# The last two half experts of a dense layer: 1024 tokens through seven block products instead of plain matmuls, the last 512 tokens plain at the end

## The chip, the core and the metric

The kernel runs on one core of a Trainium2 chip. Five engines work side by side, each through its own instructions in the order in which they stand: TensorE (PE) multiplies into PSUM banks, VectorE (DVE), ScalarE (ACT) and GpSimd (POOL) work on elements, and SP, ACT and POOL issue DMA transfers. The metric is the time of one execution on the device in microseconds (us); the less the better.

## The reference, cut to what matters

Three parts follow one another: a local attention with summary keys, a mixture of eight experts in which every token goes through every expert, and a second mixture in which each token goes through one expert. The change is in the second part and in the start of the third.

```python
x = attention(q, k, v)                    # 1536 tokens x 512
# dense part: P is the Sinkhorn-scaled softmax of the gate
for e in range(8):                        # w1[e]: 512 x 1024, w2[e]: 1024 x 512
    out += P[:, e:e + 1] * (np.maximum(x @ w1[e], 0) @ w2[e])
x = out
# routed part
e_idx = np.argmax(x @ w_gate, axis=1)
for e in range(8):                        # only the tokens that chose e
    ye = np.maximum(x[mask] @ w1[e], 0) @ w2[e]
    out[mask] = gate_w[mask, None] * eom[mask, e, None] * ye
```

## The kernel before, in words

All products are made of three matmuls each: every float32 operand is split into a high part, which is rounded (a cast on ACT, L472, L584 or L1755), and a low part, which is the rest (a subtraction on DVE, L473, L585 or L1758), and hi\*hi, lo\*hi and hi\*lo are added in one PSUM bank.

**The dense part** (`DenseMoe`) takes the eight experts in 16 halves `hx` of 512 hidden features. It handles halves 0 and 1, and 14 and 15, in a plain way: for groups of 384 tokens, `mm1` makes the hidden features (four blocks of 128, each 12 matmuls of 384 columns, L605), ACT takes their relu and high part (L612), DVE the low part (L613), and `mm2` makes one output tile of 128 tokens from 12 matmuls of 512 columns (L625), which DVE adds to that tile's sums (`acc`, L637). Halves 2 to 13 go in a Strassen scheme: sets of 512 tokens, both products of each set cut into 2 x 2 blocks of 256, and seven block products instead of eight. The seven of the first product are `s1` to `s7`, those of the second `z1` to `z7`; each is 12 matmuls of 256 columns for each of two halves (L678), 168 matmuls per set for both products. `TURNS` interleaves the `z` products of one set with the `s` products of the next. Weights and tokens are added up before they are multiplied: `weights` makes the sums and splits them, and `FIRSTS` (W1) and `SECONDS` (W2) say at which turn. The sums of the output leave SBUF at once: POOL issues DMAs that add them to a table in DRAM (`x2d<-acc`, L842).

After the last set its seven `z` products run between the plain matmuls of half 14; then the tiles are fetched back to SBUF (`reload`, L653) and get the plain contributions of halves 14 and 15. `done(i)` follows the last of tile i.

**The routed part** begins inside that. `Routing` has per tile a `flip` (PE transposes, L1289, copied to `r_xt`), the `logits` (L1298, copied to `r_lg`, L1299), and per run of tiles `choose`, `ranks`, `place`, `gates`, which sort the tokens by expert. Constants (`r_ilo` to `r_desc`, L1246) come from POOL's iotas (L1244). Two *early* slots of 128 tokens are chosen from the first `TILES` tiles, so that their work fills the end of the dense part; the rest is planned when all 12 tiles are there. `invert` (L1465) turns ranks into token numbers, POOL gathers the rows (`xg`, L1764), `flip_x` transposes them (L1782), and a slot goes through `mm1` and `mm2` of its expert (L1791) with weights of 1 MB loaded to a ring of three buffers `raw` (L1741). The function `late_steps` says in which order and with how many steps between them these run, `merge` threads them between the steps of the dense part.

## Time and profile before

| what | value |
|---|---|
| time, median of 3 runs | 1302.24 us (1301.32 to 1302.99) |
| time of the profiled execution | 1303.32 us |
| its span | 1301.2 us |
| PE busy | 1281.5 us (98%) |
| DVE, ACT, POOL busy | 840.3, 731.4, 356.5 us |

The span is from the first to the last instruction in the trace; 2.1 us of the profiled execution lie around it. The busy share of an engine counts the time in which it had an instruction in work.

### The profile page before, as it was taken

How to read it: one execution, taken by the hardware profiler on the slowest of the kernel's cores; microseconds unless marked ns; L12 is line 12 of the kernel's file. 1: busy time of each engine (PE TensorE's matmuls, PEld its weight loads, DVE VectorE, ACT ScalarE, POOL GpSimd, SP SyncE). 2: the span in 40 equal slices, each digit the busy share in tenths (PEclk: the TensorE clock that was granted, in tenths of full speed). 3: DMA queues.
4: the chain of work that ended last, by engine and by line, in shares of the span. 5: the costliest groups of instructions: out<-in, count | busy, mean ns of one | idle time of the engine just before them, and what ended most of it. 6: DMA issues, size and time to landing. Idle time of an engine off the chain costs nothing. (4 is left out here: it accounts for less than half of the span.)

```text
span 1301.2 us, 26457 instructions
## 1 busy us (share of the span) xinstructions
PE 1281.5 (98%) x10041; PEld 1205.7 (93%) x10041; DVE 840.3 (65%) x1673; ACT 731.4 (56%) x1511; POOL 356.5 (27%) x369
## 2 busy tenths in 40 slices
PE   8999999999999999999999999999999999999997
PEld 7888888999999999999999999999999998888886
DVE  6754595777778687787777787867643347514261
ACT  5764323667767677677677776767632114324362
POOL 6652005323324242333232332422210001111110
PEclk9999999999999999999999999999999999999999
DMA  9850227778889798888897888979571128114450
GB/s 218 194 123 10 89 106 283 197 192 179 194 192 198 182 211 170 226 167 211 186 200 186 177 199 192 204 176 218 81 181 34 65 82 277 64 56 141 142 194 22
DMA packets 163176, 208.84 MB, mean 160 GB/s; under 512 B 47199, under 2 KB 96351, under 8 KB 163040
## 3 DMA queue, kind: packets, MB, share of 16 engines
q1 hardware_dynamic: 114192, 138.36, 34.4%
q0 software_dynamic: 48848, 68.70, 29.7%
q8 instruction: 81, 1.33, 0.4%
q14 instruction: 55, 0.45, 0.1%
HBM read 151.18 MB, written 56.62 MB: 160 GB/s over the span
## 5 line engine op out<-in xcount | busy, mean ns | idle before, releaser
L842 POOL DMA_DIRECT2D x2d<-acc x144 | 172.8, 1243 | 453.7 <-ACT acc L837 169.6
L678 PE MATMUL bank<-hi,hlo 128*128 128x256 f32 x672 | 190.0, 283 | 0.3 <-DVE hlo L713 0.3
L678 PE MATMUL bank<-lo,hhi 128*128 128x256 f32 x672 | 189.9, 283 | 0.0
L678 PE MATMUL bank<-hi,hhi 128*128 128x256 f32 x672 | 189.5, 282 | 0.0
L678 PE MATMUL bank<-Tlo,hi 128*128 128x256 f32 x576 | 162.9, 283 | 0.0
L678 PE MATMUL bank<-Thi,lo 128*128 128x256 f32 x576 | 162.6, 282 | 0.0
L678 PE MATMUL bank<-Thi,hi 128*128 128x256 f32 x576 | 162.1, 281 | 0.0
L678 PE MATMUL bank<-hi,acc 128*128 128x256 f32 x672 | 133.7, 282 | 0.0
L678 PEld LDWEIGHTS bank<-hi,hhi 128*128 128x128 f32 x672 | 127.9, 190 | 0.3 <-DVE acc L862 0.2
L678 PEld LDWEIGHTS bank<-hi,hlo 128*128 128x128 f32 x672 | 127.4, 190 | 0.5 <-DVE hlo L713 0.5
L678 PEld LDWEIGHTS bank<-lo,hhi 128*128 128x128 f32 x672 | 127.4, 190 | 0.0
L678 PE MATMUL bank<-xhi,hi 128*128 128x256 f32 x432 | 121.4, 281 | 0.7 <-ACT t L772 0.7
L678 PE MATMUL bank<-xlo,hi 128*128 128x256 f32 x432 | 121.4, 281 | 0.0
L678 PE MATMUL bank<-xhi,lo 128*128 128x256 f32 x432 | 121.3, 281 | 0.0
L678 PEld LDWEIGHTS bank<-hi,acc 128*128 128x128 f32 x672 | 109.8, 190 | 0.0
L678 PEld LDWEIGHTS bank<-Thi,hi 128*128 128x128 f32 x576 | 109.0, 189 | 0.0
L678 PEld LDWEIGHTS bank<-Thi,lo 128*128 128x128 f32 x576 | 108.6, 188 | 0.0
L678 PEld LDWEIGHTS bank<-Tlo,hi 128*128 128x128 f32 x576 | 108.3, 188 | 0.0
L713 DVE TENSOR_TENSOR hlo<-t,hhi 128x512 fp32r<-128x512 f32 x144 | 97.0, 685 | 14.2 <-ACT hhi L705 13.4
L705 ACT CAST hhi<-t 128x512 fp32r<-128x512 f32 x144 | 88.1, 619 | 23.7 <-DVE t L807 17.4
L837 ACT ACTIVATE acc<-acc,P 128x256 f32<-128x256 f32 x216 | 96.7, 502 | 3.5 <-DVE acc L879 2.7
L612 ACT ACTIVATE hhi<-bank 128x384 fp32r<-128x384 f32 x64 | 31.4, 491 | 119.4 <-PE bank L605 119.2
(315 smaller groups left out, 3446.0 us busy)
## 6 DMA issues: line engine op xcount, KB each, us to landing
x2d<-acc POOLq DMA_DIRECT2D x147, 256.0 KB, 5.4
Thi<-td SPq DMA_DIRECT2D x144, 256.0 KB, 3.8
Tlo<-td SPq DMA_DIRECT2D x144, 256.0 KB, 4.1
raw<-in_moe_w_dram POOLq DMA_DIRECT2D x88, 256.0 KB, 5.6
raw<-in_moe_w_dram SPq DMA_DIRECT2D x20, 1024.0 KB, 5.9
raw<-in_moe_w_dram SPq DMA_DIRECT2D x40, 256.0 KB, 4.2
x2d<-acc SPq DMA_DIRECT2D x21, 256.0 KB, 2.4
vw<-in_v_dram SPq DMA_DIRECT2D x32, 120.0 KB, 3.6
```

The source lines that it names most:

```text
L612: nc.scalar.activation(out=hhi[:, c], in_=ps, func=ACTF.Relu)
L678: self.nc.tensor.matmul(bank[:, 256 * f:256 * f + 256], x[:, o:o + 128], y[:, k], start=first and n == 1, stop=n == 12, skip_group_check=True,
L705: nc.scalar.copy(hi, src)
L713: nc.vector.tensor_tensor(out=lo, in0=src, in1=hi.bitcast(F32), op=ALU.subtract)
L837: nc.scalar.activation(out=out[:, s], in_=src[:, s], func=ACTF.Copy, scale=self.P[:, i, hx // 2:hx // 2 + 1],)
L842: nc.gpsimd.dma_start(out=self.sums[n:n + 256, 256 * dh:256 * dh + 256].rearrange("(c p) d -> p c d", p=128), in_=out.rearrange("p (c d) - ...
```

## The change

Halves 14 and 15 now go through the Strassen scheme too, but for the first two of the three sets, that is for tokens 0 to 1023 (`sets` lists the sets, `FULL` is the last half with three). What the last 512 tokens (tiles 8 to 11) need from these halves is left to `rest`, called P for half 14 and R for half 15: four blocks `mm1_rest` of P (12 matmuls of 512 columns each) with the seven leftover `z` products of the last set between them, then four `mm2` tiles of P, four blocks of R, four tiles of R. In a short set the W2 sums are made in another order and earlier (`SECONDS_SOON`, from the turn of `z1` instead of `z6`), the W1 sums for what follows later (`FIRSTS_LATE`), and the W1 weights of half 15 are loaded by SP, not POOL. Tile 8 is fetched to a buffer of its own, `spare`. Tiles 0 to 7 are final when the leftover products are, so their flips and logits stand between the plain matmuls of `rest`, and the early slots are chosen from eight tiles instead of nine, in one `choose` instead of two. Nine tiles were stored twice to DRAM, eight are now stored once. A flip is copied by ACT alone. The buffers of the slots' weights other than the first two `raw` are set up only after the last product with W1 of R.

```diff
-    FIRST, LAST = 2, 13
+    FIRST, FULL, LAST = 2, 13, 15
...
+        self.sets = [
+            (hx, j) for hx in range(self.FIRST, self.LAST + 1)
+            for j in range(self.NS if hx <= self.FULL else self.NS - 1)
+        ]
...
+    SECONDS_SOON = (
+        "B11", "sumT1", "sumT3", "T3", "sumT2", "T2", "sumT4", "T1", "B21", "T4", "B22",
+    )
+    FIRSTS_LATE = {**FIRSTS, "s1": (), "s2": ("A11", "A12"), "z7": ("sumS1",)}
...
+    def rest(self, u, behind, loads, done, plain):
...
+        self.homes[8] = self.spare
+        self.reload((8, 1, 2))
+        for c in range(4):
+            yield u
+            for _ in self.mm1_rest(P, c, h[P][c]):
+                yield u
+            for turn in order[:(2, 3, 2, 0)[c]]:
+                for _ in behind[turn]():
+                    yield u
+            order = order[(2, 3, 2, 0)[c]:]
+            if c == 2:
+                for g in (1, 2):
+                    self.renew(g, F32)
+                self.later += [partial(self.split, 2, P, n) for n in range(4)]
+                self.later += [partial(self.reload, (10, 0, 3, 11, 9, 4, 5, 6, 7))] + loads(1, R)
+                self.later += [partial(done, i) for i in range(8)]
+                plain()
+        for t in range(4):
+            for _ in tile_of(P, t):
+                yield u + 1
+            if t:
+                self.split(1, R, t - 1)
+                self.load(2, R, t - 1)
+        for c in range(4):
+            yield u + 2
+            for _ in self.mm1_rest(R, c, h[R][c]):
+                yield u + 2
...
+        done("x")
+        for t in range(4):
+            for _ in tile_of(R, t):
+                yield u + 3
+            done(8 + t)
...
-    EARLY, TILES = 2, 9
+    EARLY, TILES = 2, 8
...
-        nc.scalar.copy(xt[:, 0:2], tr[:, 0:2])
-        nc.vector.tensor_copy(xt[:, 2:4], tr[:, 2:4])
+        nc.scalar.copy(xt, tr)
...
+            yield from tiles(0, T, 4, 2)
             routing.totals(T)
-            routing.ranks(6, T - 6)
+            routing.ranks(0, T)
             run(routing.early_experts())
...
+            while "x" not in finished:
+                yield
+            acc_stack.close()
+            moe2.begin(pool(m2_stack, "m2c", "left"))
+            moe2.load()
+            yield
             yield from routing.invert(T, X)
```

The order of the instructions moves on DVE and ACT in the places below (line numbers of the changed kernel are 6 to 66 higher than those of the same line before).

On DVE, the end of the last set's `z` products. Before, the low parts of W2 of half 14 (`lo`) stand ahead of the routing constants:

```order
L473 TENSOR_TENSOR lo_12415<-raw,hi_12414 128x512
L473 TENSOR_TENSOR lo_12423<-raw,hi_12422 128x512
L473 TENSOR_TENSOR lo_12430<-raw,hi_12429 128x512
L473 TENSOR_TENSOR lo_12437<-raw,hi_12436 128x512
L613 SCALAR_TENSOR_TENSOR hlo<-bank_12418,hhi 128x384
L1246 CAST r_ilo<-r_iota 128x128
L1246 CAST r_ihi<-r_iota 128x19
L1254 CAST r_ihalf<-r_ihi 1x17
```

Now the constants, then the low parts of W2 (L482), which P's first tile needs; the row ahead of these is the sum of `z3` (L904):

```order
L1311 CAST r_ilo<-r_iota 128x128
L1311 CAST r_ihi<-r_iota 128x20
L1319 CAST r_ihalf<-r_ihi 1x18
L1320 TENSOR_SCALAR r_ihalf<-r_ihalf 1x18
L1322 CAST r_half<-r_ihalf 1x18
L1324 SCALAR_TENSOR_TENSOR r_odd<-r_half,r_ihi 1x18
L1311 CAST r_tok<-r_iota 128x12
L1311 CAST r_desc<-r_iota 128x8
L1331 MEMSET r_unit 128x8
L1335 MEMSET r_run 128x8
L1340 MEMSET r_fresh 1x2
L482 TENSOR_TENSOR lo_13565<-raw,hi_13564 128x512
```

The four low parts have moved from ahead of the eight constants to behind them.

On ACT, the first early slot: `xthi` is its token block, the `whi` casts are its W2 and then the second slot's W1, `r_xt` the copies of the flips of the last tiles, and `h` the relu of the slot. Before:

```order
L1774 CAST xthi<-bank_13608 128x512
L612 ACTIVATE hhi<-bank_13601 128x384
L1755 CAST whi_12489<-raw_13392 128x1024 x2
L1755 CAST whi_12491<-raw_12493 128x1024 x2
L1291 COPY r_xt<-bank_13687 128x256
L1755 CAST whi_13716<-raw_12494 128x1024 x2
L1291 COPY r_xt<-bank_13746 128x256
```

Now:

```order
L1821 CAST whi_13987<-raw_13562 128x1024 x2
L1821 CAST whi_13989<-raw_13563 128x1024 x2
L1840 CAST xthi<-bank_14102 128x512
L1821 CAST whi_13558<-raw_13995 128x1024 x2
L1821 CAST whi_13560<-raw_13562 128x1024 x2
L1356 COPY r_xt<-bank_14147 128x512
L1821 CAST whi_14158<-raw_13563 128x1024 x2
L1356 COPY r_xt<-bank_14194 128x512
L1821 CAST whi_14160<-raw_13995 128x1024 x2
```

The order from `xthi` on is the same but for one `hhi`. What moved is `flip_x` on PE, which `xthi` waits for: 42 matmuls of the dense part stood between it and the slot's first product, and 6 do now, with the first late flip.

On DVE, the same slot, where `r_lg` copies logits, `L1313` and `L1377` begin a `choose`, and `ht0lo` and `ht1lo` are the low parts of the hidden features that the slot's second product needs. Before:

```order
L1758 TENSOR_TENSOR wlo_13717<-raw_12494,whi_13716 128x1024 x2
L1292 COPY r_xt<-bank_13746 128x256
L1758 TENSOR_TENSOR wlo_13719<-raw_13392,whi_13718 128x1024 x2
L1299 COPY r_lg<-bank_13769 128x16
L1292 COPY r_xt<-bank_13781 128x256
L1775 TENSOR_TENSOR xtlo<-bank_13793,xthi 128x512
L1299 COPY r_lg<-bank_13802 128x16
L1775 TENSOR_TENSOR ht0lo<-bank_13808,ht0hi 128x512
L1775 TENSOR_TENSOR ht1lo<-bank_13817,ht1hi 128x512
L1313 TENSOR_REDUCE r_m<-r_lg 128x3
```

Now, first from `xtlo` to the beginning of `choose`, and then from its last rows on:

```order
L1841 TENSOR_TENSOR xtlo<-bank_14102,xthi 128x512
L643 SCALAR_TENSOR_TENSOR acc_110<-bank_14095,P,acc_110 128x512
L1824 TENSOR_TENSOR wlo_13559<-raw_13995,whi_13558 128x1024 x2
L1824 TENSOR_TENSOR wlo_13561<-raw_13562,whi_13560 128x1024 x2
L1824 TENSOR_TENSOR wlo_14159<-raw_13563,whi_14158 128x1024 x2
L1363 COPY r_lg<-bank_14188 128x16
L1824 TENSOR_TENSOR wlo_14161<-raw_13995,whi_14160 128x1024 x2
L1363 COPY r_lg<-bank_14216 128x16
L1363 COPY r_lg<-bank_14235 128x16
L1841 TENSOR_TENSOR xtlo<-bank_14252,xthi 128x512
L1363 COPY r_lg<-bank_14261 128x16
L1377 TENSOR_REDUCE r_m<-r_lg 128x4
```

```order
L1396 TENSOR_REDUCE r_o<-r_f 128x4
L1390 TENSOR_TENSOR r_run<-r_run,r_oh 128x8 x2
L1841 TENSOR_TENSOR ht0lo<-bank_14284,ht0hi 128x512
L1841 TENSOR_TENSOR ht1lo<-bank_14293,ht1hi 128x512
```

The low parts `ht0lo`, `ht1lo` have moved from ahead of `choose` to behind it. The copy `r_lg` of the first flipped tile stands behind three pairs of `wlo`, that of the second behind a fourth.

## Rows read from the trace of the kernel before

**Rows 1.** The page, busy time of the engines (share of the span, instructions).

```profile
PE 1281.5 (98%) x10041; PEld 1205.7 (93%) x10041; DVE 840.3 (65%) x1673; ACT 731.4 (56%) x1511; POOL 356.5 (27%) x369
```

**Rows 2.** Windows: from:to, length, busy time of each engine (instructions), clock, DMA share, GB/s.

```profile
956.00:1014.50 58.50, 58.50 (x299) 53.37 (x298) 23.90 (x47) 13.78 (x28) 2.83 (x7) 1.00 0.39 104
...
1130.50:1290.00 159.50, 159.46 (x771) 131.17 (x772) 53.81 (x63) 66.31 (x102) 23.83 (x24) 1.00 0.34 115
```

**Rows 3.** Windows, L678 alone: PE busy (matmuls), weight loads, clock.

```profile
300.00:400.00 100.00, 100.00 (x839) 100.00 (x838) 1.00 0.83 189
```

**Rows 4.** Windows, L625 alone, in the plain part of half 14.

```profile
956.00:1014.50 58.50, 29.26 (x120) 22.40 (x120) 1.00 0.39 104
```

**Rows 5.** The chain that ended last, slots: start, us, what.

```profile
1152.26 5.50 PE bank L1791 x24
```

**Rows 6.** Waits of PE from 935 us to the end: us in total, times, longest.

```profile
PE bank L1782 <- DMA xg<-x2d,r_gidxf: 0.4, 1, 0.4
PE bank L1820 <- DVE xtlo L1775: 0.2, 1, 0.2
```

**Rows 7.** Waits of PE from 200 to 935 us.

```profile
PE bank L678 <- ACT t L772: 0.7, 1, 0.7
```

**Rows 8.** DMA issues of POOL at L457, issue to landing of 88.

```profile
DMA to landing us min/median/max: 2.7/5.4/8.1
```

**Rows 9.** Timeline, POOL, ACT at a set's start: start, us, engine, line, operation.

```profile
881.93 3.35 POOL L457 DMA_DIRECT2D raw<-in_moe_w_dram  x4
...
887.02 0.62 ACT L584 CAST hi<-raw 128x512 fp32r<-128x512 f32 x1
```

**Rows 10.** Timeline at the end of z3: PE, ACT, POOL, DVE; [idle before, releaser].

```profile
955.99 0.33 PE L605 MATMUL bank<-xhi,hi 128*128 128x384 f32 x1
...
957.62 2.59 DVE L473 TENSOR_TENSOR lo<-raw,hi 128x512 fp32r<-128x512 f32 x4 [1.79 <-ACT hi L472]
...
959.62 0.23 POOL L1244 IOTA r_iota<- 128x128 int32 x1
...
960.13 0.55 DVE L613 SCALAR_TENSOR_TENSOR hlo<-bank,hhi 128x384 fp32r<-128x384 f32 x1
...
960.60 0.21 DVE L1246 CAST r_ilo<-r_iota 128x128 f32<-128x128 int32 x1
...
962.38 0.17 DVE L1246 CAST r_desc<-r_iota 128x8 f32<-128x8 int32 x1 [0.24 <-POOL r_iota L1244]
```

**Rows 11.** Windows, PE, early in the span: PE busy (matmuls), clock, DMA share, GB/s.

```profile
18.00:19.00 1.00, 1.00 (x13) 0.50 1.26 202
...
20.00:21.00 1.00, 1.00 (x8) 0.58 0.90 126
```

**Rows 12.** Timeline of PE there.

```profile
17.52 2.83 PE L98 MATMUL bank<-ident,kn 128*64 128x128 f32 x24 [3.19 <-issue]
```

**Rows 13.** Windows, PE, after its last matmul.

```profile
1294.00:1295.00 1.00, 0.00 (x0) 1.00 0.06 16
...
1296.00:1297.00 1.00, 0.00 (x0) 1.00 0.48 184
```

**Rows 14.** Timeline of DVE, `choose` of six tiles, its first and last rows.

```profile
1050.44 0.20 DVE L1313 TENSOR_REDUCE r_m<-r_lg 128x6 f32<-128x48 f32 x1
...
1052.09 0.77 DVE L1326 TENSOR_TENSOR r_run<-r_run,r_oh 128x8 f32<-128x8 f32 x4
```

**Rows 15.** Timeline of DVE, totals of nine tiles and the input of `invert`.

```profile
1072.19 0.17 DVE L1402 TENSOR_SCALAR r_ni<-bank 128x8 int32<-128x8 f32 x1
...
1077.29 0.17 DVE L1456 TENSOR_TENSOR r_val<-r_ohhi,r_gate 128x18 f32<-128x18 f32 x1
```

**Rows 16.** Timeline of ACT and DVE in the early slots; each stands for pairs alike.

```profile
1102.55 2.00 ACT L1755 CAST whi<-raw 128x1024 fp32r<-128x1024 f32 x2
...
1103.73 2.35 DVE L1758 TENSOR_TENSOR wlo<-raw,whi 128x1024 fp32r<-128x1024 f32 x2
```

**Rows 17.** DMA issues of SP at L1741, issue to landing of 20.

```profile
DMA to landing us min/median/max: 4.9/5.9/8.0
```

More of the change, by code (lines that the diff above doesn't have):

```diff
@@ L666, in tiles_of_group, with mm1_rest @@
         return self.tiles(hx, range(3), 3 * g, part)
+    def mm1_rest(self, hx, c, block):
+        nc = self.nc
+        hhi, hlo = block
+        whi, wlo = self.w[1, hx, c]
+        ps = self.psum("m1", [128, 512])
+        xhi, xlo = (t[1][:, :, 256:768] for t in self.x)
+        n = 0
+        for k in range(4):
+            for w, x in ((whi, xhi), (whi, xlo), (wlo, xhi)):
+                nc.tensor.matmul(
+                    ps, w[:, 128 * k:128 * k + 128], x[:, k], start=(n == 0), stop=(n == 11)
+                )
+                n += 1
+            if k < 3:
+                yield
+        nc.scalar.activation(out=hhi, in_=ps, func=ACTF.Relu)
+        nc.vector.scalar_tensor_tensor(
+            out=hlo, in0=ps, scalar=0.0, in1=hhi.bitcast(F32), op0=ALU.max, op1=ALU.subtract
+        )
     def multiply(self, bank, a, b, first):
@@ L975, in new_seconds @@
                 self.later += [None] + loads(1, hx + 1)
-            else:
-                self.later += [partial(self.split, 2, hx, c) for c in range(4)]
+            elif n == 2:
+                for what in self.SECONDS_SOON:
+                    self.later += [partial(self.weights, 2, hx, what), None]
+            elif n == 10:
+                self.later += loads(1, hx + 1)
         def tiles(hx, n=1):
@@ L990, in tiles @@
                             self.rescale(t)
-                    new_seconds(hx)
+                        new_seconds(hx, 0)
+                    else:
+                        self.later += [partial(self.split, 2, hx, c) for c in range(4)]
         for u, self.goal in self.opening():
@@ L1058, in pieces @@
                     self.load(2, n, c)
-                if behind:
-                    for _ in rest((2, 3, 1, 0)[c]):
-                        yield i
-                    if c == 2:
-                        behind = None
-                        new_seconds(hx)
-                        self.later += [partial(self.reload, range(12))]
-                m = len(waiting) if hurry else 1 + (len(waiting) + c > 3)
-                for _ in tiles(hx, m):
+                for _ in tiles(hx, 1 + (len(waiting) + c > 3)):
@@ L1069, in pieces, with tile_of @@
                     yield i
             waiting = self.tiles_of_group(hx, g)
-            if (hx, g) == (HX - 1, NG - 2):
-                done("x")
-        for _ in tiles(HX - 2, 3):
-            yield len(units)
+        yield from self.rest(len(units), behind, loads, done, plain)
+    def rest(self, u, behind, loads, done, plain):
+        order = [t for t in self.TURNS if t in behind]
+        assert self.turn % 9 == 1
+        P, R = self.LAST + 1, self.LAST + 2
+        h = {P: [self.hs[n] for n in (1, 2, 3, 5)], R: [self.hs[n] for n in (0, 4, 1, 2)]}
+        def tile_of(hx, t):
+            o = slice(128 * t, 128 * t + 128)
+            parts = [
+                (tuple(x[:, o] for x in h[hx][c]), self.w[2, hx, c]) for c in range(4)
+            ]
+            yield
+            yield from self.mm2(hx, 8 + t, parts)
+        self.homes[8] = self.spare
[25 more added lines that the diff above has]
+                yield u + 2
+            if c == 0:
+                self.split(1, R, 3)
+                self.load(2, R, 3)
+            else:
+                self.split(2, R, c - 1)
+        self.split(2, R, 3)
+        done("x")
[3 more added lines that the diff above has]
+            done(8 + t)
@@ L2058, in wait, with tiles @@
                     yield
-            def tiles(i, n, w):
+            def tiles(i, n, first, w):
+                yield from wait(first)
                 for j in range(i, i + n):
@@ L2063, in tiles @@
                         yield
+                    routing.flip(j)
                     yield from wait(w)
[L2065 to L2066 removed]
                     routing.logits(j)
[L2068 removed]
                 routing.choose(i, n)
[L2070 to L2079 removed]
+                yield from wait(4)
+            yield from tiles(0, T, 4, 2)
             routing.totals(T)
[L2081 removed]
+            routing.ranks(0, T)
             run(routing.early_experts())
```

136 lines of the change are left out of this document (58 added, 78 removed).

## The prediction

> **What bounds the kernel now.** The page's busy times come first: PE has work in 1281.5 of 1301.2 us, the next engine (DVE) in 840.3 [rows 1]. The windows tell whether that holds stage by stage: in the plain part of half 14 PE is busy in 58.50 of 58.50 us, in the slots behind the dense part in 159.46 of 159.50 [rows 2]. The list of waits has, between 935 us and the end, two for PE, 0.4 and 0.2 us [rows 6]; before that one of 0.7 [rows 7]. So the dense part costs what its matmuls cost, a saved matmul is saved time, and each new wait of PE is lost time. The questions are how many matmuls go, and where PE must now wait.
>
> **Prices of matmuls.** A 256-column one of the block products: 100 us / 839 = 0.1192 us [rows 3]. One of 512 columns: 5.50 / 24 = 0.229 [rows 5]. In the plain part of half 14, 299 matmuls fill 58.5 us [rows 2], 120 of them of 512 columns [rows 4], two the last of `z3`; the other 177 have 384 columns: (58.5 - 120 x 0.229 - 0.24) / 177 = 0.174.
>
> **What goes.** Halves 14 and 15 took 2 x 4 x 4 x 12 = 384 matmuls of 384 columns (66.8 us) and 2 x 12 x 12 = 288 of 512 (66.0), 132.8 together. Now they take four sets of 168 (672 x 0.1192 = 80.1) and, for 512 tokens, 2 x (48 + 48) = 192 of 512 columns (44.0), 124.1. That is **-8.7**. The leftover `z` products are the same seven. The two waits of PE at the gather and at the late part of the tokens go or are in the new ones below: **-0.6**. One tile less in the early ranks and `invert`, and one `ranks` call instead of two: some matmuls of 4 to 24 columns, between 0 and 0.5, **-0.3**. Sum -9.6.
>
> **What comes.** I follow the order of each engine and put the traced durations on it.
>
> *Short sets.* The casts of W2 now stand on ACT ahead of the copy of an `s` bank. POOL issues the four W2 loads of a set from 881.93 on, and the cast that needs the first stood at 887.02 [rows 9], 5.1 us later; a load takes 5.4 us at the median, 2.7 to 8.1 [rows 8]. A cast that is asked for earlier waits for its load, and the copy behind it with it, and PE with that. Nothing if loads are quick; 8.1 - 5.4 = 2.7 if one in the two sets is the slowest. I take 0.45 for each set, nearer to the low end, since only what is left over after the slack of several turns counts: **+0.9** (0 to 2.7).
>
> *z6 and z5* follow each other directly on the same bank between P's blocks, with an ACT copy between. The trace has such a wait once, 0.7 [rows 7]: **+0.65** (0 to 0.7).
>
> *P's first tile.* This is the largest. Before, the end of `z3` can be timed: the next matmul starts at 955.99; POOL's first iota ends at 959.85, as POOL first issues `z3`'s sums; the first constant could be made then, but starts at 960.60 behind an `hlo` of 0.55 that has no such place now; from it to the end of the last constant it takes 960.60 to 962.55, 1.95 us [rows 10]. So: 3.86 + 0.1 + 1.95 = 5.9 us after `z3`, and 0.65, a quarter of the 2.59 of four `lo` [rows 10], for the first low part of W2, which now stands behind the constants: 6.6. PE has, after `z3`, 12 matmuls of P's last block and the first of the tile, which needs only high parts: 13 x 0.229 = 3.0. PE waits **+3.6**. Behind the waiting matmul stands all of PE's work. Before, the four `lo` ran at 957.62, ahead of the constants, and nobody waited. It costs nothing only if the constants are ready 3.6 us earlier (0 to 3.6).
>
> *Tile 2's flip and logits* wait for W1 of R, whose loads SP issues behind reloads that wait for the sums in DRAM; with the gap above most of it is covered: **+0.35** (0 to 2).
>
> *Totals and `invert`.* `choose` of six tiles takes from 1050.44 to 1052.86 [rows 14]; its last four rows are 0.77, so eight tiles take some 2.8 and four 1.9. Between the last logits and the totals PE has 12 matmuls (2.75), against 0.25 + 2.8: +0.3. From the totals to the input of `invert` DVE took 1072.19 to 1077.46, 5.3 us [rows 15], with eight tiles in one go some 0.7 more, a `lo` of R's W2 before it; PE has 24 matmuls (5.5) for it: +0.7. The next `lo` comes behind all this: +0.5. Together **+1.5** (0 to 3.5).
>
> *The first early slot.* Six matmuls now separate `flip_x` from the slot. Count from its end. On ACT: `xthi` 0.62 (the cast of rows 9), two `whi` pairs of 2.00 [rows 16], the copy `r_xt` 0.62: 5.2 us. PE gets through 6 + 6 matmuls and a flip (0.35) in 3.1 and stands at the logits: 2.1. On DVE: `xthi`, `xtlo`, the sums of the last tile, then three `wlo` pairs of 2.35 [rows 16] and the first `r_lg`: 0.62 + 0.7 + 0.75 + 7.05 + 0.2 = 9.3. PE, at 5.2, does logits (0.8), a flip and nine matmuls (2.1), stands at 8.4 for the PSUM bank that `r_lg` frees: 0.9. The second `r_lg` stands behind a fourth pair, whose load SP issues when the first pair is done (4.4). With 5.0 us for the load, `whi` 2.0, the last `wlo` 1.2: 12.8; PE is there at 11.8: 1.0. Together **+4.0**. A load of 1 MB takes 4.9 to 8.0, median 5.9 [rows 17]; I take the low end since the DMA share in the nearest plain stretch is 0.39 against 0.83 in the block products [rows 2, 3]; with 8.0 it is 7.0.
>
> *`choose` before `ht0lo`.* After the last logits PE transposes `h` (0.9) and does two matmuls (0.45), while DVE copies, chooses (1.9) and makes `ht0lo` (0.7): 0.25 + 1.9 + 0.7 = 2.85 against 1.35: **+1.5** (0.5 to 1.7).
>
> Sum of costs: 0.9 + 0.65 + 3.6 + 0.35 + 1.5 + 4.0 + 1.5 = 12.5. With -9.6: **+2.9**. The profiled execution took 1303.32, that is 2.1 more than its span and 1.1 more than the median; on it 1306.2, on the median of 1302.24: **1305.1**. Behind the early slots PE is bound by its matmuls before and after, so nothing is given back there.
>
> **The rivals.** A measurement of this kernel tells 0.2% (2.6 us) from no change, so *faster* is below 1299.6, *slower* above 1304.8.
>
> *1. P's first tile does not wait.* If the constants are made while `z3` runs, the 3.6 and with it the 0.35 go: 1305.1 - 3.95 = 1301.1, not slower. It decides at whether the first low part is there 3.0 us after `z3`. For it: POOL's iotas need nothing of `z3`. Against it: the constants stand behind the sums of `z3` on DVE, and POOL's idle time did not help before. With the small terms (short sets, totals) at the low end as well, another 2.4 go, and 1.1 of the rest: 1297.6.
>
> *2. The clock falls in that gap.* Early in the span PE stood still for 3.19 us, and what followed at 17.52 [rows 12] ran at a granted clock of 0.50 and came back only within the window from 20 to 21 us (0.58) [rows 11]: some 3.3 us at 1.2 instead of 2.4 GHz, in which half the work, 1.65 us, is lost. Against it: after its last matmul at the end PE stands idle with the clock at 1.00 in the windows from 1294 to 1297 [rows 13]. The gap of 3.6 at P's first tile lies just above the 3.19. The 0.35 behind it would be covered, so +1.3: 1306.4, and 1307.5 with a longer gap. The Trainium skill, page "TensorE: Matmul & The Clock Gate", section "HAM oscillation — how this bites in real kernels", says that a PE which waits too long for data is throttled and starts its next stretch cold; the rows early in the span agree (0.50 after 3.19 us).
>
> *3. Late loads.* If the load in the first slot takes 8.0 us, +3.0; if a set's load is the slowest, +1.8: 1308.1 to 1309.9.
>
> *4. The gain doesn't come.* If the 512-column plain products were slower than 0.229, or a set longer than 20.0 us; against it stands that both run without waits in the trace. It gives at most +2 and is in the range.
>
> **How the numbers follow.** The forecast has 0.40 (own range 1302.5 to 1307.5: the small terms at their ends), in which 0.24 is slower, 0.14 no change, 0.02 faster. Rival 1 has 0.24: 0.13 no change and 0.11 faster, as 1301.1 lies between, and 1297.6 beyond. Rival 2 has 0.16: 0.14 slower, 0.02 no change. Rivals 3 and 4 have 0.08, of which 0.04 no change. The rest, 0.12, is for waits that I take to be in series and that overlap: the slot's 4.0 and 1.5 both hang on DVE, and without them it is 1299.6, counted as faster. Faster 0.25, no change 0.33, slower 0.42. The range is 1297.6, rival 1 with the low ends, to 1309.9, rival 3.
>
> **What would show it.** In the profile after: four more sets with PE at 100% and 0.119 us a matmul, less 0.45 us twice. A wait of PE of about 3.6 us for a low part (`lo`, L482) at P's first tile; none there is rival 1; a granted clock of about 0.50 in the microseconds after it is rival 2. Waits for `r_xt` (about 2) and for `r_lg` (0.9 and 1.0) in the first slot, and for `ht0lo` (1.5). The slots behind must take as long as before. Wrong would be the forecast above all if DVE has the low parts of W2 in time, or if the logits do not wait in the slot: then the saved 9.6 us come through.

## The result and the profile after

The changed kernel takes 1315.52 us (median of 6 runs, 1312.89 to 1317.48), the kernel before 1303.46 in the same comparison (6 runs, 1301.32 to 1305.80): a ratio of 1.0089 [1.0072, 1.0106], slower by 12.1 us. The forecast was 1305.1, slower by 2.9, with a range up to 1309.9: the sign is right, the size is not. The profiled execution took 1316.05 us with a span of 1314.3, 13.1 above that of before.

The page of the changed kernel, busy times, stands beside [rows 1]:

```profile
PE 1281.3 (97%) x10227; PEld 1205.4 (92%) x10227; DVE 879.2 (67%) x1712; ACT 786.1 (60%) x1605; POOL 385.3 (29%) x398
```

PE is busy as long as before (1281.3 against 1281.5 us) although the matmuls of the change cost less. So not only were 13 us of idle time added (33.0 against 19.7); the saved work has also been filled up with something that counts as busy. The waits of PE from 870 to 1165 us, where [rows 6] had two (total, times, longest):

```profile
PE bank L1362 <- ACT r_xt L1356: 4.0, 1, 4.0
PE bank L631 <- DVE lo L482: 3.4, 1, 3.4
PE bank L703 <- ACT acc L881: 2.2, 3, 0.9
PE bank L703 <- DVE acc L887: 1.9, 1, 1.9
PE bank L1857 <- DVE ht0lo L1841: 1.4, 1, 1.4
PE bank L1411 <- DVE r_run L1390: 0.8, 1, 0.8
PE bank L703 <- ACT t L783: 0.6, 2, 0.3
```

With three of 0.2 these are 14.9 us. Windows of 1 us on PE (busy, matmuls, granted clock, DMA share, GB/s) show the rest, behind the three longest waits:

```profile
977.00:978.00 1.00, 0.00 (x0) 1.00 0.45 172
...
979.00:980.00 1.00, 1.00 (x6) 0.50 0.00 0
...
982.00:983.00 1.00, 1.00 (x9) 0.84 1.15 174
1052.00:1053.00 1.00, 0.00 (x0) 1.00 1.11 203
...
1054.00:1055.00 1.00, 1.00 (x4) 0.50 1.14 288
...
1057.00:1058.00 1.00, 1.00 (x4) 0.80 0.77 102
...
1109.00:1110.00 1.00, 1.00 (x5) 0.50 0.95 352
...
1115.00:1116.00 1.00, 1.00 (x8) 0.78 0.55 172
```

In the windows 977 and 1052, in which PE stands, the clock is still 1.00. From 979, 1054 and 1109 on, the granted clock is 0.50, that is 1.2 instead of 2.4 GHz, for three, three and six whole windows and part of one more. Taking what the clock lacks of 1.00, times the busy share, window by window: 1.7 + 1.7 + 3.2 = 6.6 us. PE is "busy" in them, at half speed. Then 14.9 + 6.6 - 9.6 (the forecast's saving) = 11.9 us, against 13.1 in the span.

The 6.6 is that of the one profiled execution. The mean granted clock of all six is 0.992 or 0.993 (mean 0.9928); that of the kernel before is 0.995 to 0.998 in 42 executions of the comparisons below (mean 0.9963; two more, which took over twice as long, are left out here). An estimate from these is (0.9963 - 0.9928) x 1313 = 4.6 us for the clock in the median of 12.1.

Where each long wait comes from. The block products of half 14 first: rows of ACT, then of DVE (start, us, line, operation, and in brackets the idle time before and who ended it).

```profile
948.35 0.62 ACT L590 CAST hi<-raw 128x512 fp32r<-128x512 f32 x1 [2.82 <-DMA raw<-in_moe_w_dram]
...
950.06 0.57 ACT L881 COPY acc<-bank 128x512 f32<-128x512 f32 x1
```

```profile
972.04 0.69 DVE L575 TENSOR_TENSOR s<-raw 128x512 f32<-128x512 f32 x1 [1.53 <-DMA raw<-in_moe_w_dram]
...
977.26 0.69 DVE L887 TENSOR_TENSOR acc<-bank,acc 128x512 f32<-128x512 f32 x1
```

The copy that frees the bank (L881) stands behind a cast that waited 2.82 us for a W2 load; PE then waits 0.63. In the same way L887, on DVE, stands behind the sums of W1 of half 15; PE waits 1.93. SP issued three of the four loads behind its fetches of `T`:

```profile
961.98 0.43 SPq L534 DMA_DIRECT2D Tlo<-td  x1
962.58 2.03 SPq L466 DMA_DIRECT2D raw<-in_moe_w_dram  x3
```

P's first tile, on DVE and PE:

```profile
1050.44 0.23 DVE L1311 CAST r_ilo<-r_iota 128x128 f32<-128x128 int32 x1 [4.47 <-POOL r_iota L1309]
...
1052.36 0.69 DVE L482 TENSOR_TENSOR lo<-raw,hi 128x512 fp32r<-128x512 f32 x1
...
1053.10 0.50 PE L631 MATMUL bank<-lo,hhi 128*128 128x512 f32 x1 [3.44 <-DVE lo L482]
```

DVE stood still for 4.47 us before the first constant, and the low part of W2 that PE needs stands behind all of them. And the first early slot, on SP, ACT and PE:

```profile
1097.61 0.37 SPq L1807 DMA_DIRECT2D raw<-in_moe_w_dram  x1
...
1106.47 1.99 ACT L1821 CAST whi<-raw 128x1024 fp32r<-128x1024 f32 x2 [2.17 <-DMA raw<-in_moe_w_dram]
...
1108.37 0.58 ACT L1356 COPY r_xt<-bank 128x512 f32<-128x512 f32 x1
...
1109.00 1.89 PE L1362 MATMUL bank<-r_w,r_xt 128*128 128x16 f32 x8 [4.02 <-ACT r_xt L1356]
```

A load that was issued at 1097.61 let the cast start at 1106.47, 8.9 us later, and the copy of the flip stands behind two such casts. The slots behind run as before: 145.78 of 146.00 us busy, as in [rows 2].

```profile
1157.00:1303.00 146.00, 145.78 (x703) 119.57 (x703) 50.54 (x58) 61.13 (x94) 19.95 (x20) 1.00 0.34 119
```

### The profile page after: what moved, and what is told of

Same layout as the page of the kernel before. It is cut to its first block, busy times and chain, and to the rows that moved or that the text cites. A ratio compares the mean times of both kernels' runs of the same rounds, so it can differ in the third digit from the quotient of the medians.

```text
span 1314.3 us, 27146 instructions
## 1 busy us (share of the span) xinstructions
PE 1281.3 (97%) x10227; PEld 1205.4 (92%) x10227; DVE 879.2 (67%) x1712; ACT 786.1 (60%) x1605; POOL 385.3 (29%) x398
## 5 line engine op out<-in xcount | busy, mean ns | idle before, releaser
L867 POOL DMA_DIRECT2D x2d<-acc x160 | 192.2, 1247 | 514.8 <-ACT acc L862 338.4
L703 PE MATMUL bank<-hi,hhi 128*128 128x256 f32 x748 | 211.5, 283 | 3.5 <-DVE acc L887 1.9
L703 PE MATMUL bank<-hi,hlo 128*128 128x256 f32 x748 | 211.7, 283 | 0.3 <-DVE hlo L738 0.3
L703 PE MATMUL bank<-lo,hhi 128*128 128x256 f32 x748 | 211.6, 283 | 0.0
L703 PE MATMUL bank<-Tlo,hi 128*128 128x256 f32 x640 | 181.0, 283 | 0.0
L703 PE MATMUL bank<-Thi,hi 128*128 128x256 f32 x640 | 180.3, 282 | 0.6 <-ACT t L783 0.6
L703 PE MATMUL bank<-Thi,lo 128*128 128x256 f32 x640 | 180.6, 282 | 0.0
L703 PEld LDWEIGHTS bank<-hi,hhi 128*128 128x128 f32 x748 | 142.5, 190 | 4.4 <-DVE acc L887 2.1
L703 PEld LDWEIGHTS bank<-hi,hlo 128*128 128x128 f32 x748 | 142.1, 190 | 0.5 <-DVE hlo L738 0.5
L703 PE MATMUL bank<-lo,acc 128*128 128x256 f32 x372 | 105.1, 283 | 0.0
```

The source lines that it names most:

```text
L703: self.nc.tensor.matmul(bank[:, 256 * f:256 * f + 256], x[:, o:o + 128], y[:, k], start=first and n == 1, stop=n == 12, skip_group_check=True,
L867: nc.gpsimd.dma_start(out=self.sums[n:n + 256, 256 * dh:256 * dh + 256].rearrange("(c p) d -> p c d", p=128), in_=out.rearrange("p (c d) - ...
```

## The experiments

All leave the computation as it is; those with unused matmuls say so. The kernel before stood between 1302.6 and 1304.1 us in their comparisons. "Less" or "more than the change" compares medians, 1315.52 for the change; executions of one kernel lie up to 9 us apart, so a difference of 2 or 3 us between two medians of four to seven is not shown by them alone.

**The constants behind the low parts of W2.**

```diff
+                self.later += [plain]
                 self.later += [partial(self.reload, (10, 0, 3, 11, 9, 4, 5, 6, 7))] + loads(1, R)
                 self.later += [partial(done, i) for i in range(8)]
-                plain()
```

> The routing constants (and the other work of plain) are emitted after the four splits of W2 of P, so that the four low parts stand ahead of the constants on DVE as they did before the change; nothing else moves. Theory A (each wait is lost by itself, and the clock falls in it): the wait of 3.4 us at P's first tile goes and the 1.7 us of low clock behind it too, 5.1 us faster. Theory B (the wait only covers a second chain, the reloads and the loads of W1 of R that SP issues behind them, which land at the same absolute time): a wait of 4 to 5 us shows up at the flips or logits of tiles 0 to 2 instead, the clock falls there, and the time is within 1 us of the changed kernel's.

Measured: 1320.76 us (1319.51 to 1323.97), ratio 1.0134 [1.0114, 1.0154]: slower than the change by 5 us, which neither theory said; theory B has the mechanism. The wait for `lo` is gone, and others are there that hang on the loads of W1 of R: ACT stands 6.45 us at one,

```profile
1060.32 0.62 ACT L481 CAST hi<-raw 128x512 fp32r<-128x512 f32 x1 [6.45 <-DMA raw<-in_moe_w_dram]
```

and PE waits 4.6 us for the `r_lg` copy that stands on DVE behind that cast's low part, and 2.1, 1.7 and 1.7 at three other places. The clock stays at 0.50 from 1062 to 1071, nine windows on end. So at P's first tile the constants were the wait that ended last, but without it PE stands a few steps later, at the reloads and W1 of R.

**The loads of W1 of R ahead of most reloads as well.** The constants stand behind them here, and so does the load of the gate's weights, which is made with them.

```diff
-                self.later += [partial(self.reload, (10, 0, 3, 11, 9, 4, 5, 6, 7))] + loads(1, R)
+                self.later += [partial(self.reload, (10, 0))] + loads(1, R) + [plain]
+                self.later += [partial(self.reload, (3, 11, 9, 4, 5, 6, 7))]
                 self.later += [partial(done, i) for i in range(8)]
-                plain()
```

> As the run with the constants later, and W1 of R is loaded by SP ahead of seven of the nine late reloads. Theory A: 5.1 us faster, as without the loads moved. Theory B: only with both chains shortened does the time go down; 3 to 5 us faster than the changed kernel, and at least 2 us faster than the run that moves the constants alone. If neither is so, a third chain (the reload of tile 0 or 3) ends last.

Measured: 1320.06 us (1315.34 to 1323.81), ratio 1.0111 [1.0078, 1.0145]. Neither theory holds: it is not faster than the change. Five waits are 2 us or longer behind 1050 us: `r_lg` 3.1, `r_xt` 2.4, `r_val` 2.1, the gate's weights 2.0 (an effect of this edit alone), the reload of a tile 2.0. With W1 of R moved ahead, a reload and the gate's weights are late instead.

**The first slot's order: the flip's copy ahead of the casts.**

```diff
-                if s == 0 and i in (0, 2):
+                if s == 0 and i in (3, 5):
...
+                    if j == T:
+                        moe2.split(0, 1)
...
-            moe2.split(0, 1)
-            yield from wait(6)
             finished.add("early")
```

> In the first early slot the split of its last block of W2 is emitted after the first late tile's logits, not before its flip, and the two splits of the second slot's W1 two steps later, so that the copy of the flipped tile on ACT stands ahead of the cast that waits for the late load. Theory A: the wait of 4.0 us for the copy shrinks to under 1, the clock does not fall behind it (3.2 us), 5 to 7 us faster. Theory B (PE is then held by the same late loads one product further on): the wait moves to the second slot's weights or the first slot's second product and under 2 us are gained.

Measured: 1311.65 us (1307.70 to 1314.63), ratio 1.0061 [1.0041, 1.0081], 3.9 us less than the change, between the two theories. The wait of 4.0 for `r_xt` is gone, 0.7 (`r_lg`) and 1.3 (`xtlo`) are new, and the clock keeps 1.00 at 1109; it falls at 1120 instead, behind the three waits of 0.7, 1.3 and 1.5 (`ht0lo`), which stand within 6 us. The six executions spread from 1307.70 to 1314.63 with mean clocks from 0.996 to 0.991; less what each lacks of a clock of 1.00, times its span, they are 1301.2 to 1302.8, an estimate, as the clocks are rounded to 0.001. By it the spread is nearly all the clock.

**Unused matmuls in the two gaps.** 15 of 512 columns ahead of P's first tile and 17 ahead of the first late logits, whose result nobody reads: the engines do the same work, with PE not idle.

```diff
+        self.idle(15)
         for t in range(4):
             for _ in tile_of(P, t):
...
+                    if j == T:
+                        ps = psum("t", [128, 512])
+                        hi, lo = moe2.w[0, 0]
+                        for m in range(17):
+                            nc.tensor.matmul(
+                                ps, hi[:, 0, 0:128], hi[:, 1], start=(m == 0), stop=(m == 16)
+                            )
```

> Nothing is moved; PE gets work that no one uses where it stands still: 15 matmuls of 512 columns (3.4 us) ahead of P's first tile and 17 (3.9 us) ahead of the first late tile's logits. The engines and transfers that PE waits for do the same as before, so PE goes on at the same moment. Theory A (the granted clock falls because PE stood still): the clock stays at 1.00 in both places, and the kernel is 4.9 us faster (1.7 + 3.2) although it does 32 matmuls more. Rival (the clock falls for another reason, or the low clock hides behind other waits): no change, or slower by what the matmuls overrun.

Measured: 1312.51 us (1310.87 to 1320.14), ratio 1.0083 [1.0055, 1.0111]: the median is 3.0 less, but the interval covers that of the change, so a gain is not shown by the times, only that 32 matmuls more cost nothing that can be measured. The profiled execution, 1310.87, has a span 5.3 shorter. The clock is 1.00 from 1050 to 1060 and from 1100 to 1110, where the change had 0.50. It falls at another place (windows of PE):

```profile
1085.00:1086.00 1.00, 0.80 (x7) 1.00 1.04 403
1086.00:1087.00 1.00, 0.91 (x7) 1.00 1.03 399
1087.00:1088.00 1.00, 1.00 (x8) 0.98 1.06 408
1088.00:1089.00 1.00, 1.00 (x5) 0.50 1.04 387
```

There PE does `invert`, twice eight matmuls of four columns between those of R's tile, and no wait longer than 0.2 us stands within the 8 us before it. In the two gaps the idle time was thus part of the loss twice: as a wait, and as the cause of the slow stretch behind. The traces of the other kernels bear this out: at P's first tile, with the wait of 3.4 us left empty, the clock fell in four of five (not with W1 on POOL, below), and with it filled in none of three; at `r_xt`, with a wait of 3.9 to 4.4 left empty, in four of four, and filled in the one that there is it did not.

**W1 of half 15 loaded by POOL again.**

```diff
-            (nc.sync if hx == self.FIRST or (which, hx) == (1, self.LAST) else nc.gpsimd).dma_start(
+            (nc.sync if hx == self.FIRST else nc.gpsimd).dma_start(
```

> Undoes one part of the change alone: the W1 loads of half 15 go to POOL's queue again, not SP's. The changed kernel's PE waits in the block products behind 940 us are 4.8 us in sum, of which 1.9 for the weights sums of W1 of half 15, whose loads SP issues at 955.4 and 962.6 behind its fetches of token blocks and which land up to 9 us later. Theory A (SP's order makes these loads late): they are issued earlier from POOL, and the 1.9 us go. Theory B (the four buffers come free too late, whichever queue it is): the wait stays between 1 and 3 us.

Measured: 1312.01 us, a single execution, span 1309.9; its time alone decides nothing, its waits are what counts. The wait at L887 falls from 1.9 to 0.5 us, those at L881 grow from 2.2 to 3.9; the casts of ACT wait 8.7 us for loads where they waited 7.1. The wait for W1 goes, as theory A has it, and the waits for W2 grow by as much, which neither theory said. The clock differs too, and not by the length of a wait: the one at P's first tile is unchanged, and no fall follows it (timeline, then windows of PE).

```profile
1049.61 0.50 PE L631 MATMUL bank<-lo,hhi 128*128 128x512 f32 x1 [3.42 <-DVE lo L482]
```

```profile
1050.00:1051.00 1.00, 1.00 (x6) 1.00 1.15 280
1051.00:1052.00 1.00, 1.00 (x6) 1.00 0.99 341
```

**The same loads on SP, but threaded between the W2 sums.**

```diff
+                after = {"sumT1": 0, "T3": 1, "B21": 2, "B22": 3}
                 for what in self.SECONDS_SOON:
                     self.later += [partial(self.weights, 2, hx, what), None]
-            elif n == 10:
-                self.later += loads(1, hx + 1)
+                    if what in after:
+                        self.later.append(loads(1, hx + 1)[after[what]])
```

> In the short sets each load of the next W1 is emitted as soon as the sums of W2 have read its buffer, instead of all four behind the last sum. Theory A (the buffers come free one by one, and the loads could start some 5 us earlier): the loads of half 15 are issued before 962, the wait of 1.9 us for its sums goes, and the clock does not fall there (1.7 us): 2 to 4 us less in the profile. Theory B (the loads share the DMA rings with the sums' transfers, and their landing is what is slow): issued earlier, but the wait stays above 1 us.

Measured: 1315.24 us, a single execution, span 1313.3. SP issues the four loads between 953.2 and 968.1 instead of between 955.4 and 964.6, the first earlier, the last later. L887 has 0.9 us and L881 3.2: together 4.1, as in the change. The clock does not fall there, as theory A has it, but the waits do not go.

**The W2 sums at the old turn.**

```diff
-                        if short and turn == "z1":
+                        if short and turn == "z6":
```

> Undoes one part alone: in a short set the sums and splits of W2 begin at the turn of z6 again, not of z1. Theory A (begun at z1 they stand on ACT ahead of copies, wait for their loads, and hold PE): the waits of PE for an ACT copy of L881 and L783 (0.6 and 0.3 in each of two sets, 1.9 in sum) go. In exchange the buffers come free later, and the wait for the sums of W1 grows from 1.9 to 3 or more. Theory B (these waits have nothing to do with the order of the sums): 1.9 us stay.

Measured: 1311.65 us, a single execution, span 1309.9. The waits of the block products shrink from 4.8 to 1.6 us (0.9 at L887, and the 0.7 between `z6` and `z5`), and the clock is 1.00 from 940 to 1000. The 1.9 us go, as theory A has it; the wait for W1, which it had growing to 3 or more, shrinks to 0.9. So it was the early turn of the W2 sums that cost most of the 4.8, by asking for loads that were not there. The two kernels that follow differ in this turn alone and agree: 4.8 against 1.7 us.

**Slot order, `choose` behind `ht0lo`, and 15 unused matmuls at P's first tile.**

```diff
+        self.idle(15)
...
-                if s == 0 and i in (0, 2):
+                if s == 0 and i == 3:
...
-                if s == 0 and i in (2, 4):
+                if s == 0 and i in (0, 2, 4):
...
+                    if j == T:
+                        moe2.split(0, 1)
+                if i:
+                    yield from wait(3)
                 routing.choose(i, n)
...
-            moe2.split(0, 1)
-            yield from wait(6)
```

> Three edits together: the order of the splits in the first early slot (its own last block behind the first late logits, the second slot's behind the transposes of h), the early slot's low parts ahead of the choice of the last four tiles, and 15 unused matmuls ahead of P's first tile in place of PE's wait there. If the waits behind P are lost one by one, as theory A has it, the waits for the flipped copy (4.0), the late logits, and ht0lo (1.4) go, the low clock behind P's first tile and in the slot (1.7 and 3.2) too: 8 to 10 us faster than the changed kernel, about 1306. It stays slower than the kernel before if what is left, 3.4 us at P's first tile and some 5 to 6 in the short sets, is more than the 8.7 us of saved matmuls can pay.

Measured: 1311.42 us (1308.83 to 1315.07), ratio 1.0069 [1.0048, 1.0090]: 4.1 less than the change, not 8 to 10. In the profiled execution (1308.83) the clock is 1.00 from 870 to 1165 us, after a wait of 1.9 at L887 as well, and 10.7 us of waits are left, 4.8 of them in the block products. The four executions lie 6 us apart at mean clocks of 0.996 to 0.998: not every difference between executions is the clock.

**The same with the W2 sums at `z6`.** The diff is the last one and that of the turn together.

> The three edits of the run with the slot's order, the choice and the dummy matmuls, and the W2 sums of the short sets begun at z6 as in the look with the later sums. What should be left of waits behind 940 us is 0.9 and 0.7 in the block products, 3.4 at P's first tile (filled by dummies), about 2 at totals and invert and about 2 in the slot, some 9 us, with the clock at 1.00. Against 9.6 us saved that is the time of the kernel before within 0.3% (1300 to 1307). Theory A is wrong in its sum if it stays above 1309. The rival, that the saved matmuls are not worth 8.7 us, would also leave it above 1309, with waits as small as said.

Measured: 1308.34 us (7 runs, 1304.53 to 1313.76), ratio 1.0050 [1.0032, 1.0069]: above the 1300 to 1307 of the expectation, below the 1309 that would have refuted it. The profiled execution is the fastest, 1304.53 with a span of 1302.7, only 1.5 above that of before. Its stretch as a whole, and its longest waits:

```profile
940.00:1160.00 220.00, 212.02 (x1390) 1.00 0.63 163
```

```profile
PE bank L1421 <- DVE r_run L1400: 1.7, 2, 0.9
PE bank L1372 <- DVE r_lg L1373: 1.4, 2, 0.9
PE bank L1858 <- DMA xg<-x2d,r_gidxf: 1.1, 1, 1.1
PE bank L712 <- DVE acc L896: 1.0, 1, 1.0
```

All waits together are 7.7, the unused matmuls 15 x 0.229 = 3.4: 7.7 + 3.4 - 9.6 = 1.5, which is what the span shows. The seven runs also show the clock's price: two with a mean clock of 0.991 took 1312.74 and 1313.76, five with 0.995 to 0.997 took 1304.53 to 1309.14 (mean 1306.7): 6.5 us between the means.

**The kernel before, with the constants ahead of the low parts of W2.** The one move by itself, without any of the rest.

```diff
-            if hx == self.LAST + 1 and g == 1:
-                plain()
...
+                        plain()
```

> The kernel before with one thing of the change: the routing constants are emitted ahead of the splits of W2 of half 14, right behind z3. Nothing else differs. Theory A: the first low part is ready 6.6 us after z3 instead of 2.3, PE needs it 4.2 us after z3 and waits 2.4 us; nothing behind gives it back, since the plain part there has slack in its loads: 2.4 us slower, and 1.7 more if the clock falls in a wait of that length. Theory B (such a wait only covers later ones): within 1 us of the kernel before.

Measured: 1305.40 us (8 runs, 1304.51 to 1307.44) against 1302.86, ratio 1.0022 [1.0012, 1.0032], 2.5 us slower. PE waits, and the clock does not fall (waits, then windows):

```profile
PE bank L625 <- DVE lo L473: 1.5, 1, 1.5
```

```profile
961.00:962.00 1.00, 0.00 (x0) 1.00 0.95 197
962.00:963.00 1.00, 0.93 (x4) 1.00 1.15 281
963.00:964.00 1.00, 1.00 (x6) 1.00 1.09 346
```

The span rose by 1.7, as the wait says; the median rose by more, and no trace shows what the rest is. That the constants' place costs PE a wait is shown.

**All edits, without unused matmuls.** The W2 sums at `z6`, the slot order and `choose` of above, the constants behind the low parts, tile 0 flipped after tiles 1 and 2, and W1 of R split a tile later.

```diff
+                self.later += [plain]
...
-                self.later += [partial(done, i) for i in range(8)]
-                plain()
+                self.later += [partial(done, i) for i in (1, 2, 0, 3, 4, 5, 6, 7)]
...
-            if t:
-                self.split(1, R, t - 1)
-                self.load(2, R, t - 1)
+            if t > 1:
+                self.split(1, R, t - 2)
+                self.load(2, R, t - 2)
...
```

> No dummy matmuls; the slot's order, the choice and the later W2 sums of the short sets as before, and the tail's first chain taken apart: the constants behind the low parts of W2 of P, the flips in the order 1, 2, 0, 3 to 7 (tile 0 is fetched last of the three), and the splits of W1 of R one tile later, so that DVE does not stand at a load while logits wait to be copied. Theory A with its chains: of the 11 us of waits and dummies in the profile of the run with all but the gap, 3.4 at P's first tile and 1 at r_lg go, some 7 us stay against 9.6 saved; 1300 to 1303, as fast as the kernel before or up to 0.2% faster. If the clock still falls in two or three places of a microsecond of waiting, 1304 to 1307.

Measured: 1310.71 us (1307.82 to 1312.22), ratio 1.0059 [1.0046, 1.0072]: slower than either expected range. 10.3 us of waits, the longest now behind the reload of tile 9 (DVE, then PE):

```profile
1053.51 0.75 DVE L643 SCALAR_TENSOR_TENSOR acc<-bank,P,acc 128x512 f32<-128x512 f32 x1 [5.21 <-DMA acc<-x2d]
```

```profile
1054.49 1.04 PE L1363 MATMUL bank<-r_w,r_xt 128*128 128x16 f32 x8 [2.10 <-DVE r_lg L1364]
```

and 6.8 us lost to a clock of 0.50 from 1056 and from 1087. The mean clock of the six executions is 0.9907, against 0.9966 for the kernel before beside them: an estimate from these is (0.9966 - 0.9907) x 1310 = 7.7 us for the clock, of the 8.1 between the medians. By this estimate the kernel would be about level with the one before if the clock held as it does there. The profiled execution of the last kernel with unused matmuls is 6.0 us faster with the same matmuls and 15 more: no wait of its own is above 1.1, and the clock held.

**Only the edits at P and R of that kernel.** The diff is that of the last one; the W2 sums, the slot and `choose` are as in the change.

> The changed kernel with the tail's first chain alone taken apart: the constants behind the low parts, flips in the order 1, 2, 0, 3 to 7, and the splits of W1 of R one tile later. The constants alone made it slower, since DVE then stood at the load of W1 of R (4.6 us) ahead of the copy of logits. Theory A with its chains: with that copy no longer behind the load, the 3.4 us at P's first tile and the 1.7 us of low clock go and at most 1 to 2 us come back at the fetch of tile 0 or 3: 3 to 5 us faster than the changed kernel. Theory B (whatever is taken away at this place, the loads of W1 of R end last): a wait of 3 us or more at the flips, the logits or R's first block, and within 2 us of the changed kernel.

Measured: 1314.93 us (1313.86 to 1319.20), ratio 1.0091 [1.0076, 1.0106]: as the change, and within the 2 us of theory B, though no single wait reaches its 3 us. The wait at P's first tile is gone but for 1.1, `r_lg` has 2.3 and `r_xt` in the slot 1.7, and in the profiled execution 11.6 us go to the clock.

None of the kernels beats the one before. The edits left to do are those in the list of the kernel with 7.7 us of waits; that it would pass with these waits gone, at a clock that holds without unused matmuls, is arithmetic and was not shown.

**The account of all profiled executions.** Waits are the sum of PE's list of waits from 870 to 1165 us, "clock" is the loss as worked out above from windows of 1 us, unused matmuls have 0.229 us each, and 9.6 is the forecast's saving (for the kernel before with one move only the 0.6 of its old waits is taken off).

| kernel | waits | clock | unused | sum less 9.6 | span above 1301.2 |
|---|---|---|---|---|---|
| the change | 14.9 | 6.6 | - | 11.9 | 13.1 |
| constants later | 16.9 | 10.1 | - | 17.4 | 17.5 |
| constants and loads | 17.9 | 11.4 | - | 19.7 | 20.6 |
| slot order | 12.9 | 4.6 | - | 7.9 | 9.9 |
| unused in two gaps | 8.8 | 1.7 | 7.3 | 8.2 | 7.8 |
| W1 on POOL | 16.7 | 1.7 | - | 8.8 | 8.7 |
| W1 threaded | 15.3 | 4.2 | - | 9.9 | 12.1 |
| W2 sums at `z6` | 12.1 | 6.2 | - | 8.7 | 8.7 |
| slot, choose, unused | 10.7 | 0 | 3.4 | 4.5 | 5.9 |
| and W2 sums at `z6` | 7.7 | 0 | 3.4 | 1.5 | 1.5 |
| before, one move | 2.2 | 0 | - | 1.6 | 1.7 |
| all edits | 10.3 | 6.8 | - | 7.5 | 7.7 |
| edits at P and R | 13.4 | 11.6 | - | 15.4 | 16.2 |

Spans from 1302.7 to 1321.8 come out within 2.2 us, seven of the thirteen within 0.4, with one saving for the twelve that have the change. On average these twelve lie 0.7 above the sum, so 8.9 would fit a little better than 9.6.

The falls of the clock in these traces, from 870 to 1165 us, are 24. Eleven last two or three whole windows at 0.50 and cost 1.5 to 1.7 us each, eleven last five or six and cost 2.5 to 3.4, one lasts nine and one thirteen, for 5.0 and 6.5; the mean is 2.7.

## Why the prediction was wrong

| term of the sum | forecast | measured |
|---|---|---|
| matmuls and old waits gone | -9.6 | -9.6 fits all spans within 2.2, -8.9 best |
| short sets | +0.9 | 4.1 (1.93, 0.94, 0.63, 0.32, 0.30) |
| `z6` and `z5` | +0.65 | 0.68 |
| P's first tile | +3.6 | 3.44 |
| tile 2's flip and logits | +0.35 | 0 |
| totals and `invert` | +1.5 | 0.98 |
| first early slot | +4.0 | 4.02 |
| `choose` before `ht0lo` | +1.5 | 1.37 |
| the granted clock | 0 | 6.6 |

**The step that failed** is rival 2 and its place outside the sum. It named the fall of the clock, with [rows 11, 12] as its measure, but looked for it in one gap only, priced it at 1.65, took 0.35 off as covered, and gave it 0.16; the top of the range, rival 3, has late loads alone and no fall with them. It came behind three waits, of 1.93, 3.44 and 4.02 us, and cost 6.6 in the profiled execution, 3.2 of it in the slot, where the clock came back only after six windows. That is two thirds of the miss there (13.1 against 2.9); by the estimate of 4.6 for all six executions it is half of the miss of the medians (12.1 against 2.9).

The evidence that I held against it was cut off too early. [rows 13] end at 1297, with the clock at 1.00; the same view of the kernel before goes on, with PE still idle:

```profile
1297.00:1298.00 1.00, 0.00 (x0) 0.71 0.21 78
1298.00:1299.00 1.00, 0.00 (x0) 0.50 0.00 0
```

So the clock falls at the idle end too, and these rows agree with [rows 11, 12] instead of speaking against them. Nor does 1.00 in the windows of a wait say that no fall follows: 977 and 1052 have it in the change. In longer waits 0.50 can be there before PE works again (1107 with W1 threaded, 1102 with the W2 sums at `z6`, both without a matmul). Two of the three waits stood in my own list of costs, and only one was asked about; the third, at L887, had no price at all. The Trainium skill, page "TensorE: Matmul & The Clock Gate", section "HAM oscillation — how this bites in real kernels", says that waits for data put PE at its half clock when the next stretch begins, each time anew; the three falls here agree, the equal waits without one (below) do not.

**Short sets** were mis-sized: 4.1 against 0.9, beyond the bound of 2.7. Of it 2.2 are the late loads of W2, the mechanism that was named, within its bound. The other 1.93 was not costed at all: W1 of half 15 is loaded by SP behind its `T` fetches and adds up on DVE ahead of the sum that frees PE's bank. I had listed the change of queue and gave it no price. The kernel with the sums at `z6` shows how the two hang together: it takes both down, to 0.9 for W1 and 0 for W2.

**The slot** came to 4.02, as forecast, by luck. The forecast had 2.1 at `r_xt` and 0.9 and 1.0 at `r_lg`; measured are 4.02 and 0. The load of the second pair of casts, which SP had issued at 1097.61, ahead of the slot, was taken as landed; it took 8.9 us to its cast, and the cast waited 2.17 with the copy `r_xt` behind it. PE then came so late that both waits for `r_lg` were covered, although the load that I did price, at 5.0, issued at 1106.25 (4.4 us after `xthi`, as forecast), took 7.2 to its cast at 1113.44. The reason for the low end, a DMA share of 0.39 in the nearest plain stretch, did not hold there: 1.06 and 1.02 in the windows from 1105 to 1107.

**Right**, each to about 0.5 us: P's first tile, also in its parts (the first low part is ready 6.5 us after `z3`, forecast 6.6), so rival 1 fell; `choose` before `ht0lo`; `z6` and `z5`; totals. The kernel before with the one move has the same wait, though shorter than expected of it (1.5, not 2.4). The saving is right to about 1 us, so rival 4 fell: in the short sets, from 1000 to 1020 us, 170 matmuls fill 20.00 us without a wait, 0.118 each, and a block of P, from 1040.90 to 1043.63, has 12 matmuls of 512 columns, 0.228 each. That tile 2 waits behind W1 of R was right as a chain, but hidden: it shows as soon as the constants move, and then costs more than they did.

## What to carry over

On a kernel whose TensorE is busy 98% of the time, ask of each new wait in the sum, not of the longest alone, whether the clock will fall behind it, and put a price with a chance on that (here, for waits of about two us and more, it mostly fell; a fall cost 1.5 to 1.7 us or 2.5 to 3.4, each in eleven of 24 cases, and 5.0 and 6.5 once). Where rows are to speak for or against a fall, read on to the end of the stretch. Where a change makes an engine ask earlier for a load, find the load in the trace first, on the queue that will issue it, and price the wait on the engine that asks and on all that stands behind it there. Moving the instruction that ends a wait pays only when the next one in that chain has slack; when it has none, as with the constants, the reloads and W1 of R, the wait moves on and may grow.

## What was not expected of the hardware

- The clock does not follow the length of one wait alone. It fell behind 1.93, 3.44 and 4.02 us in the change, but not behind 3.42 at the same place with W1 on POOL, nor behind 1.9 at the sum of `z` that L887 is in the change, in the two kernels that have unused matmuls later on and the W2 sums at `z1`, nor behind 1.5 in the kernel before with one move; with the slot order it fell behind 1.5, after two shorter waits, and at `invert` in the kernels with edits at P and R behind 0.7, 1.4 us after one of 1.1. Equal kernels thus differ from run to run (1304.53 to 1313.76), and what decides it stays open.
- It also fell without a wait longer than 0.2 us in the 8 us before: in the kernel with unused matmuls in two gaps, at 1088, behind two windows with PE busy for 0.80 and 0.91 and eight matmuls of four columns in each of two groups. The section "A second HAM failure mode: psum-queue depth-cycling" of the same page of the Trainium skill says that many small pauses between groups of matmuls can do this; the place would fit, but it is one place in one trace, no bank is waited for there, and no run here tests it.
- How long it stayed low varied: two or three whole windows in eleven of 24 falls, five or six in another eleven, nine in the kernel with the constants later, and thirteen (1111 to 1123, with pauses of PE in them) in that with only the edits at P and R. The one fall that the forecast had as its measure, some 3.3 us, is of the short kind.
- A load of 1 MB took 8.9 us from issue to the cast that used it, with the DMA share at 0.78 to 1.06; the landings of the seven loads from 1085 to 1112 us, against [rows 17] (all 20 loads of the changed kernel: 5.1, 6.8, 9.6):

```profile
DMA to landing us min/median/max: 5.1/7.0/9.6
```
